# Moving small operations and sums in a fused SSM and long-convolution kernel

## The chip, the cores and the metric

The kernel runs on one NeuronCore of a Trainium2 chip. Its five engines work side by side and wait for each other through semaphores: TensorE (PE in the profile; PEld is its loading of weights), VectorE (DVE), ScalarE (ACT), GpSimd (POOL) and SyncE (SP), which only issues transfers. ACT and POOL issue transfers too. The metric is the device time of one execution in microseconds (us). Three runs of the kernel before took 380.99, 381.09 and 382.37 us, median 381.09 us.

## What is computed

The inputs are x of 2048 rows and 1024 channels, k and v of the same shape, and the parameters of two layers. Cut to what matters:

```
g = sigmoid((x * gate_w).sum(-1, keepdims=True))

# A: a diagonal complex state-space layer
Lam = Lambda_re + 1j*Lambda_im;  Lam_bar = exp(exp(log_dt) * Lam)
B_bar = ((Lam_bar - 1) / Lam)[:, None] * (B_re + 1j*B_im)
h_t = Lam_bar * h_{t-1} + B_bar x_t
a = 2 * (h C^T).real + x * Dskip

# B: a gated long convolution
k_shift[t] = sum_i k[t - i] * shift_k[:, i]      # 4 taps
kv = k_shift * v
y = irfft(rfft(pad(kv)) * rfft(pad(ssm_k)))[:2048] + kv * ssm_D
b = x * y

out = g * a + (1 - g) * b
```

Inputs and output are bf16.

## The kernel before

**The convolution (B) comes first,** in eight chunks of 128 channels. The transform is done by matmuls with cosine and sine tables (CF, SF, NCF forward, CI, SI back), and the signal is folded first: its halves are mirrored, then added and subtracted, so that the tables need half the rows. For each chunk c:

- `taps(c)`: PE makes the four-tap sums of k; ACT copies them to the tile ks (chunks from 3 on use a packed form with the small diagonals `ident2` times `pcol2`).
- `times_v(c)`: DVE multiplies ks by v; PE mirrors the first half (`mirror`); ACT copies the mirrored half to the tile lo; DVE writes ev = ks - lo; then ks + lo is made by a transfer that adds (`gather`, on POOL's queue; in chunk 1 by DVE). Each `yield` ends one step, and the caller decides what stands between two steps.
- `fold_K(c)` or `fold_columns(c)` or `mirror_K(c)`: the same folding of the filter kernel, on PE, with ACT copying the result to eok.
- `fwd_K(c)` and `fwd_V(c)`: the transforms (PE psk and psv, ACT copies to Kh and Vh; some Kh lie in the tile BT).
- `products(c)`: DVE multiplies the spectra. In the chunk loop its operations are, in order, G = Kh*Vh (128 x 4096), wkh = Kh*Vh (128 x 3072, then gathered into G), the product into BT (128 x 4096), a second wkh, and the rest with sums and differences.
- `inverse(c)`: PE psz, ACT copies to cv, which goes to a scratch in DRAM.

The loop `for c in range(NC - 1)` handles in iteration c the products of chunk c, the transforms of c + 1 and the taps and fold of c + 2. Iteration 0 is written out apart, in the branch `if c == 0`.

**The state-space layer (A) follows,** already begun in the chunk loop (`Bu`, PE both, even and odd), with scans on DVE, the matmuls with C (`Cy`, PE psy) and the sums of both layers at the end. C is turned by complex factors first: `turn_C(pi)` makes the products on ACT or DVE and sums them with DVE or, for tiles 0, 1, 4 and 5, by gathers.

**The order is written by hand.** The helper `put` ties each operation to the one before it on its engine, so the order of calls in the program is the order on PE, DVE, ACT and on the queues of SP and POOL. The set-up operations that call `nc.gpsimd` directly are not tied. Since an engine works its list in order, an operation that waits holds up all that stands behind it. PSUM is used as four rotating tiles of two banks each (`ps2`); a tile comes free when its reader, mostly ACT, is done.

**The head** is all that comes before the loop: tables, the columns of parameters (`columns`, with `pcol`, `pcol2`, `gwb` and `ident2`), chunk 0, half of chunk 1, and `state_params`, a generator of small operations on 128 x 8 tiles (th, sq, fr, invden, the sine and cosine, lam, mlam and later factors). `raise_clock` issues matmuls on zeros ahead of the first data. `lam_diag(0)` in iteration 0 uses lam and mlam on ACT.

The profile gives line 94 (in `put`) for nearly all operations, so they are told apart by the names of their tiles.

Of the kernel before, what the change touches and what calls it, by code (L numbers as in the profile page):

```python
# [9 lines left out]
ALU = mybir.AluOpType  # L10
# [10 lines left out]
def kernel(  # L21
# [26 lines left out]
    nc = tc.nc  # L48
# [34 lines left out]
    def u4(shape, dt, name):  # L83
        return s5p["wu"].tile(shape, dt, name=name, tag="u4")
# [12 lines left out]
    def mm(o, l, r, first, last):  # L97
        put("pe", nc.tensor.matmul, o, lhsT=l, rhs=r, start=first, stop=last)
# [15 lines left out]
    def copy(o, a):  # L114
        put("dve", V.tensor_copy, o, a)
# [183 lines left out]
    for k, v in enumerate((1.0, -1.0)):  # L299
        nc.gpsimd.affine_select(out=refl[:, k], in_=refl[:, k], pattern=[[1, 128]], base=-127, channel_multiplier=1,  # L300
                                compare_op=ALU.not_equal, fill=v)
    nc.gpsimd.memset(idents[:, 1:], 0.0)
    for k, v in ((1, 1.0), (2, -1.0)):
        nc.gpsimd.affine_select(out=idents[:, k], in_=idents[:, k], pattern=[[1, 128]], base=0, channel_multiplier=-1,
# [5 lines left out]
    pcol = consts.tile([128, 3 + KS, ND], F32, name="pcol")  # L310
    gwb = consts.tile([128, ND], BF16, name="gwb")
    pcol2 = consts.tile([128, 4, ND], F32, name="pcol2")
    ident2 = consts.tile([128, 64], BF16, name="ident2")
    psp = ps2([128, 2, 512], "p")
    raise_clock(3)
    for k in range(KS):
        mm(psp[:, 1, k * ND:(k + 1) * ND], skr[:, :, k], ident[32:32 + ND, 32:32 + ND], True, True)
    hf = u4([128, 2, 512], F32, "h")
    for mt in range(2):
        ts(hf[:, mt], fr_, colm[:, mt:mt + 1], None, ALU.mult)  # L320
    copy(pcol[:, 3:], psp[:, 1, 0:KS * ND].rearrange("p (i j) -> p i j", j=ND))
    dg0 = ks_pool.tile([128, KS, 128], BF16, name="dg", bufs=1)
    for k in range(KS):
        ts(dg0[:, k], ident, pcol[:, 3 + k, 0:1], None, ALU.mult)
# [2 lines left out]
    def columns():  # L327
        mm(psp[:, 0, 0:3 * ND], prow, ident[64:64 + 3 * ND, 64:64 + 3 * ND], True, True)
        copy(pcol[:, 0:3], psp[:, 0, 0:3 * ND].rearrange("p (i j) -> p i j", j=ND))
        yield  # L330
        psp2 = ps2([128, 2, 512], "p")
        mm(psp2[:, 1, KS * ND:(KS + 1) * ND], gwr, ident[32:32 + ND, 32:32 + ND], True, True)
        for q in range(4):
            for t in range(2):
                mm(psp2[t * 64:t * 64 + 64, 1, 64 + q * ND:64 + (q + 1) * ND],
                   skr[:, q // 2 * 64:q // 2 * 64 + 64, q % 2 + 2 * t], ident[32:32 + ND, 32:32 + ND], True, True)
        yield
        copy(gwb, psp2[:, 1, KS * ND:(KS + 1) * ND])
        copy(pcol2, psp2[:, 1, 64:64 + 4 * ND].rearrange("p (i j) -> p i j", j=ND))
        tt(ident2, ident[:, 0:64], ident[:, 64:128], ALU.add)  # L340

    def dgs(c, on_dve=False):
        if c >= 3:
# [66 lines left out]
    def state_params():  # L410

        dtv = small("dtv")
        act(dtv, logdt, func=ACT.Exp)
        yield
        abv = pair("abv")
        tt(abv, bc(dtv[:, None], [128, 2, NP]), pcol[:, 1:3], ALU.mult)
        yield
        act(rv, abv[:, 0], func=ACT.Exp)
        ts(thn, abv[:, 1], 1.0 / TWO_PI, None, ALU.mult)
        ts(nthn, abv[:, 1], -1.0 / TWO_PI, None, ALU.mult)  # L420
        yield
        th = pair("th")
        copy(th[:, 0], thn)
        ts(th[:, 1], thn, float(TB), None, ALU.mult)
        sq = pair("sq")
        tt(sq, pcol[:, 1:3], pcol[:, 1:3], ALU.mult)
        fr = pair("fr")
        ts(fr, th, MAGIC, -MAGIC, ALU.add, ALU.add)
        invden = small("invden")
        tt(invden, sq[:, 0], sq[:, 1], ALU.add)  # L430
        tt(fr, th, fr, ALU.subtract)
        put("dve", V.reciprocal, invden, invden)
        yield

        fa = pair("fa")
        act(fa, fr, func=ACT.Abs)
        si, co = pair("sin"), pair("cos")
        act(si, fr, func=ACT.Sin, scale=TWO_PI)
        act(co, fa, func=ACT.Sin, bias=pih, scale=-TWO_PI)
        cs["sU"], cs["cU"] = si[:, 1], co[:, 1]  # L440
        yield

        e = pair("e", 3)
        tt(lam[:, 0], rv, co[:, 0], ALU.mult)
        tt(lam[:, 1], rv, si[:, 0], ALU.mult)
        ts(mlam, lam[:, 1], -1.0, None, ALU.mult)
        yield
        tt(rv2, rv, rv, ALU.mult)
        copy(e[:, 1], lam[:, 1])
        ts(e[:, 2], lam[:, 0], -1.0, None, ALU.add)  # L450
        ts(e[:, 0], lam[:, 0], -1.0, None, ALU.add)
        p2 = pair("p2")
        tt(p2, e[:, 1:3], pcol[:, 1:3], ALU.mult)
        p1_ = th
        tt(p1_, e[:, 0:2], pcol[:, 1:3], ALU.mult)
        tt(p2[:, 0], p2[:, 0], p2[:, 1], ALU.subtract)
        tt(p1_[:, 0], p1_[:, 0], p1_[:, 1], ALU.add)
        for o, i, f in ((mc2i, p2, -2.0), (c2r, p1_, 2.0), (mc2r, p1_, -2.0)):
            put("dve", V.scalar_tensor_tensor, out=o, in0=i[:, 0], scalar=f, in1=invden, op0=ALU.mult, op1=ALU.mult)
# [220 lines left out]
    def products(c, h=0, home=u4, by_dma=True):  # L680

        if c not in GH:
            GH[c] = spectrum("G", c)
        K, Vt, G = (x[c][h].rearrange("p c b f d -> p c b (f d)") for x in (KH, VH, GH))
        w = K.shape[3]
        T2s = kv_pool.tile([128, 4096], BF16, name="t2", tag="kvh") if c == NC - 1 else BT[3].rearrange("p c d q -> p (c d q)")
        T2 = T2s[:, h * 2048:h * 2048 + 8 * w]
        W1, W2 = (WK[:, i, h * 1536:h * 1536 + 6 * w] for i in range(2))

        def mult(a, k, room, t=None):  # L690

            full = [128, 2, 4 - a, w]
            if t is None:
                t = room.rearrange("p (c b x) -> p c b x", c=2, x=w)
            tt(t, bc(K[:, k:k + 1, a:a + 1], full), Vt[:, :, 0:4 - a], ALU.mult)
            return t

        if c == 0 and h == 0:

            for f in range(2):  # L700
                k_, v_, g_ = (x[c][h][:, :, :, f] for x in (KH, VH, GH))
                tt(g_, bc(k_[:, 0:1, 0:1], [128, 2, 4, 128]), v_, ALU.mult)
        else:
            mult(0, 0, None, G)
        yield
        n1 = mult(1, 0, W1)
        if by_dma:
            gather(G[:, :, 1:], n1)
        yield
        t2 = mult(0, 1, T2)  # L710
        yield
        n2 = mult(1, 1, W2)
        if not by_dma:
            tt(G[:, :, 1:], G[:, :, 1:], n1, ALU.add)
        if c == NC - 1:
            yield
        n3 = mult(2, 1, home([128, 4 * w], BF16, "t"))
        tt(t2[:, :, 1:], t2[:, :, 1:], n2, ALU.add)
        n2 = mult(3, 1, home([128, 2 * w], BF16, "t"))
        tt(t2[:, :, 2:], t2[:, :, 2:], n3, ALU.add)  # L720
        n1 = mult(2, 0, W2[:, 0:4 * w])
        n3 = mult(3, 0, W2[:, 4 * w:])
        tt(t2[:, :, 3:], t2[:, :, 3:], n2, ALU.add)
        tt(n1[:, :, 1:], n1[:, :, 1:], n3, ALU.add)
        yield
        tt(G[:, :, 2:], G[:, :, 2:], n1, ALU.add)
        yield
        tt(t2[:, 1], G[:, 0], t2[:, 1], ALU.subtract)
        tt(t2[:, 0], G[:, 1], t2[:, 0], ALU.add)
        if c == 0 and h == 0:  # L730
            return
        lo, hi = ((t2[:, :, :, 0:256], t2[:, :, :, 256:512]) if c > 0 else
                  [T2s[:, i * 2048:(i + 1) * 2048].rearrange("p (c b x) -> p c b x", c=2, x=256) for i in range(2)])
        to = whole[c].rearrange("p (a c b x) -> p a c b x", a=2, c=2, b=4)
        tt(to[:, 0], lo, hi, ALU.subtract)
        tt(to[:, 1], lo, hi, ALU.add)
# [363 lines left out]
    step(angles)  # L1100
    step(angles)
    step(sp)
    run(first)
    dg1 = dgs(1, True)
    load("kT", 1)
# [4 lines left out]
    fwd_V(0, (0, 1))  # L1110
    step(turns)
    taps(1, dg1)
    step(columns)
    p0 = products(0, 0)
    steps(p0, 3)
    run(columns)
    step(sp)
    tv = times_v(1)
    step(tv)
    fwd_K(0, (2, 3))  # L1120
# [15 lines left out]
    for c in range(NC - 1):  # L1136
        n, nn = c + 1, c + 2
        if c == 0:
# [16 lines left out]
            fwd_K(n, (2, 3))  # L1155
            step(p1)
            step(sp)
            fwd_V(n)
            run(p1)
            run(fold_K(nn))  # L1160
            tv = times_v(nn)
            step(tv)
            load("kn", 3)
# [14 lines left out]
            step(parts)  # L1178
        step(back)
        step(tv)  # L1180
        steps(prod, 3)
        run(tv)
        step(old)
        step(tabs)
        run(back)
# [89 lines left out]
    def turn_C(pi):  # L1275
# [9 lines left out]
        for c, f in enumerate((c2r, mc2r)):  # L1285
            if by_sum:
                act(CT[pi][:, c], CT[pi][:, c], func=ACT.Identity, scale=f[:, pi:pi + 1])
            else:
                ts(CT[pi][:, c], CT[pi][:, c], f[:, pi:pi + 1], None, ALU.mult)
            if by_sum:  # L1290
                gather(CT[pi][:, c], m[c])
                yield
        if not by_sum:
            tt(CT[pi], CT[pi], whole_m, ALU.add)

    turning = [turn_C(pi) for pi in range(NP)]
# [250 lines left out]
```

## Time and profile before

| what | value |
|---|---|
| median of three runs | 381.09 us |
| the profiled execution | 381.05 us |
| its span, first to last instruction | 379.3 us |
| PE busy | 372.4 us, 2469 matmuls |
| DVE busy | 369.3 us, 595 instructions |
| ACT busy | 309.1 us, 475 instructions |
| POOL busy | 81.2 us, 111 instructions |

The span is what the profile sees; the execution is 1.75 us longer. A row of the timeline gives the start in us from the span's start, the duration, the engine, the line, the operation, the tile written, `<-`, the tiles read, shapes, and how many such instructions follow each other; in brackets stands how long the engine sat idle before, and what ended that. Consecutive operations of one engine overlap by 0.08 to 0.1 us, since a duration runs to the last write, so steps from start to start add up and durations do not. Ends of matmuls are modelled. Numbers of buffers are left out: BT stands for four tiles that are used for several things.

### The profile page before, as it was taken

Reading aid. Unit: us, or ns where it says so; the run is one execution under the profiler, and the core shown is the slowest. Engines: PE = TensorE matmul, PEld = TensorE weight load, DVE = VectorE, ACT = ScalarE, POOL = GpSimd, SP = SyncE. Lnnn points to the kernel's source line nnn. Section 1 sums busy time; section 2 is a strip of 40 time slices with the busy share of each in tenths; the row PEclk is TensorE's granted clock in tenths of the full one; section 3 lists DMA queues with packets and bytes.
Section 4 is the critical chain, followed back from the end, with each engine's and each line's share of the span. In section 5 each row is a group of like instructions: output and inputs, shape, how many; then the busy total and the mean of one; then the engine's idle time right before and its main releaser. Section 6 shows DMA issues by size and latency. Waiting matters only on the chain.

```text
span 379.3 us, 6708 instructions
## 1 busy us (share of the span) xinstructions
PE 372.4 (98%) x2469; PEld 200.1 (53%) x2469; DVE 369.3 (97%) x595; ACT 309.1 (81%) x475; POOL 81.2 (21%) x111
## 2 busy tenths in 40 slices
PE   7999999999999999999999999999999999999996
PEld 5656357575674846644454444444445444444444
DVE  8899999999999999999999999999999999999996
ACT  5879997988979999786949999996989759937611
POOL 4011030110301103031003112122414323635000
PEclk9999999999999999999999999999999999999999
DMA  7979999999999998969998999957898999899902
GB/s 168 168 115 242 234 202 193 232 209 202 194 170 213 233 207 177 174 144 152 199 200 188 200 230 257 250 111 134 155 231 174 221 251 246 145 250 164 225 2 111
DMA packets 126547, 71.78 MB, mean 189 GB/s; under 512 B 104681, under 2 KB 107633, under 8 KB 126514
## 3 DMA queue, kind: packets, MB, share of 16 engines
q1 hardware_dynamic: 112416, 45.90, 55.7%
q0 software_dynamic: 12976, 25.17, 39.2%
q10 hardware_dynamic: 1122, 0.28, 0.5%
q8 instruction: 19, 0.31, 0.3%
q14 instruction: 14, 0.11, 0.1%
HBM read 15.48 MB, written 8.39 MB: 63 GB/s over the span
## 4 chain that ended last, share of the span: by engine, by line
DVE 42%; PE 27%; DMA 14%; issue 10%; ACT 4%; POOL 2%; SPq 0%; DVEq 0%; POOLq 0%; ACTq 0%
PE both L94 16%; DVE BT L94 12%; DMA U<-Q 10%; DVE wkh L94 8%; DVE G L94 5%; DVE W L94 3%; PE psk L94 3%; PE psz L94 2%; DMA V<-Q 2%; DVE t L94 2%; DVE ks L94 2%; DVE hb L94 2%; PE psv L94 2%; PE taps L94 1%; DMA kT<-in_B_k_dram 1%
## 5 line engine op out<-in xcount | busy, mean ns | idle before, releaser
L94 PEld LDWEIGHTS <-BT 128*128 128x128 bf16 x640 | 62.1, 98 | 48.3 <-issue 0.2
L94 PE MATMUL both<-xT,BT 128*128 128x512 bf16 x384 | 83.7, 379 | 0.0
L94 POOL DMA_DIRECT2D U<-Q x26 | 26.4, 1029 | 82.3 <-ACT Q L94 40.5
L94 PEld LDWEIGHTS <-hb 128*128 128x128 bf16 x256 | 25.0, 98 | 30.2 <-issue 0.5
L94 PEld LDWEIGHTS <-U 128*128 128x128 bf16 x252 | 24.6, 98 | 27.4
L94 PE MATMUL psy<-CT,hb 128*128 128x512 bf16 x160 | 36.8, 379 | 0.0
L94 ACT ACTIVATE Vh<-psv 128x1024 bf16<-128x1024 f32 x32 | 30.7, 1032 | 5.8 <-PE psv L94 5.8
L94 PE MATMUL psy<-CT,U 128*128 128x512 bf16 (+1 forms) x160 | 35.1, 368 | 0.0
L94 ACT ACTIVATE U<-both 128x512 bf16<-128x512 f32 x44 | 24.2, 594 | 10.0 <-PE both L94 9.7
L94 DVE TENSOR_TENSOR_SCAN W<-rv,init,A 128x256 bf16<-128x256 f32 x48 | 32.1, 729 | 0.0
L94 POOL DMA_DIRECT2D G<-wkh x8 | 9.8, 1219 | 102.6 <-DVE wkh L94 102.6
L94 ACT ACTIVATE Q<-U,lam 128x512 bf16<-128x512 bf16 (+1 forms) x52 | 29.9, 612 | 0.0
L94 PE MATMUL psk<-eok,SF 128*128 128x384 bf16 (+1 forms) x120 | 28.5, 354 | 0.0
L94 PEld LDWEIGHTS <-SF 128*128 128x128 bf16 x184 | 18.0, 98 | 18.8 <-issue 0.2
L94 PE MATMUL psz<-G,CI 128*128 128x512 bf16 x64 | 24.3, 379 | 0.0
L94 PE MATMUL psz<-G,SI 128*128 128x512 bf16 x64 | 24.3, 379 | 0.0
L94 PE MATMUL psy<-CTa,hb 128*128 128x512 bf16 x96 | 22.7, 379 | 0.0
L94 PE MATMUL taps<-dg,kT 128*128 128x128 bf16 (+1 forms) x352 | 21.7, 210 | 0.7 <-DMA kT<-in_B_k_dram 0.6
L94 PEld LDWEIGHTS <-kT 128*128 128x128 bf16 x352 | 21.1, 100 | 2.3 <-DMA kT<-in_B_k_dram 1.8
L94 DVE TENSOR_TENSOR wkh<-BT,Vh 128x3072 bf16<-128x3072 bf16 (+4 forms) x20 | 21.8, 1109 | 0.0
L94 DVE TENSOR_TENSOR wkh<-Kh,Vh 128x3072 bf16<-128x3072 bf16 (+2 forms) x16 | 21.3, 1349 | 0.0
L94 PE MATMUL psy<-CTa,U 128*128 128x512 bf16 (+1 forms) x92 | 20.8, 370 | 0.0
(230 smaller groups left out, 843.5 us busy)
## 6 DMA issues: line engine op xcount, KB each, us to landing
U<-Q POOLq DMA_DIRECT2D x26, 256.0 KB, 5.1
G<-wkh POOLq DMA_DIRECT2D x6, 768.0 KB, 8.8
cv_scr<-cv SPq DMA_DIRECT2D x16, 256.0 KB, 7.7
kn<-in_B_ssm_k_dram SPq DMA_DIRECT2D x5, 512.0 KB, 4.4
v<-in_B_v_dram SPq DMA_DIRECT2D x5, 512.0 KB, 7.1
out_dram<-m SPq DMA_DIRECT2D x8, 256.0 KB, 4.2
BT<-cv_scr SPq DMA_DIRECT2D x7, 256.0 KB, 6.6
out_dram<-BT SPq DMA_DIRECT2D x7, 256.0 KB, 2.0
```

Of the source, the lines that this page charges most:

```text
L94: i = f(*a, **kw)
```

## The change

Five places are edited.

1. In the head, `ident2` is made by POOL (a memset and two affine selects) instead of a DVE sum; the eight matmuls for `pcol2` stand right behind those for `pcol`, and ACT copies the result; `gwb` is copied by ACT, and `columns` loses a step.
2. In `state_params` a new step boundary stands behind `fr`, and one more `step(sp)` follows the angles, so that th, sq and fr come before chunk 0's folding; lam is made by two operations on POOL, mlam by ACT. The first products of chunk 0 get a step boundary more, and the second wkh stands ahead of ks times v of chunk 1.
3. In iteration 0, `fold_K(2)` stands ahead of `fwd_V(1)`.
4. In iterations 1 to 6, the last step of `times_v` (ev and its gather) stands ahead of the product into BT.
5. In `turn_C`, tiles 0 and 1 are summed by one gather of 128 x 2048 each, behind both of ACT's products, instead of two of 128 x 1024.

```
+    ident2 = consts.tile([128, 64], BF16, name="ident2")
+    nc.gpsimd.memset(ident2, 0.0)
+    for k in range(2):
+        nc.gpsimd.affine_select(out=ident2, in_=ident2, pattern=[[1, 64]], base=64 * k, channel_multiplier=-1,
+                                compare_op=ALU.not_equal, fill=1.0)
...
     for k in range(KS):
         mm(psp[:, 1, k * ND:(k + 1) * ND], skr[:, :, k], ident[32:32 + ND, 32:32 + ND], True, True)
+    for q in range(4):
+        for t in range(2):
+            mm(psp[t * 64:t * 64 + 64, 1, 64 + q * ND:64 + (q + 1) * ND],
+               skr[:, q // 2 * 64:q // 2 * 64 + 64, q % 2 + 2 * t], ident[32:32 + ND, 32:32 + ND], True, True)
...
     copy(pcol[:, 3:], psp[:, 1, 0:KS * ND].rearrange("p (i j) -> p i j", j=ND))
+    act(pcol2, psp[:, 1, 64:64 + 4 * ND].rearrange("p (i j) -> p i j", j=ND), func=ACT.Copy)
...
         mm(psp2[:, 1, KS * ND:(KS + 1) * ND], gwr, ident[32:32 + ND, 32:32 + ND], True, True)
-        for q in range(4):
-            for t in range(2):
-                mm(psp2[t * 64:t * 64 + 64, 1, 64 + q * ND:64 + (q + 1) * ND],
-                   skr[:, q // 2 * 64:q // 2 * 64 + 64, q % 2 + 2 * t], ident[32:32 + ND, 32:32 + ND], True, True)
-        yield
-        copy(gwb, psp2[:, 1, KS * ND:(KS + 1) * ND])
-        copy(pcol2, psp2[:, 1, 64:64 + 4 * ND].rearrange("p (i j) -> p i j", j=ND))
-        tt(ident2, ident[:, 0:64], ident[:, 64:128], ALU.add)
+        act(gwb, psp2[:, 1, KS * ND:(KS + 1) * ND], func=ACT.Copy)
...
         ts(fr, th, MAGIC, -MAGIC, ALU.add, ALU.add)
+        yield
...
-        tt(lam[:, 0], rv, co[:, 0], ALU.mult)
-        tt(lam[:, 1], rv, si[:, 0], ALU.mult)
-        ts(mlam, lam[:, 1], -1.0, None, ALU.mult)
+        for k, o in enumerate((co, si)):
+            put("pool", nc.gpsimd.tensor_tensor, out=lam[:, k], in0=rv, in1=o[:, 0], op=ALU.mult)
+        act(mlam, lam[:, 1], func=ACT.Copy, scale=-1.0)
...
-        if c == NC - 1:
+        if c == NC - 1 or (c, h) == (0, 0):
             yield
...
     step(angles)
     step(sp)
+    step(sp)
     run(first)
...
-    step(columns)
+    run(columns)
     p0 = products(0, 0)
     steps(p0, 3)
-    run(columns)
     step(sp)
+    step(p0)
     tv = times_v(1)
...
             step(sp)
+            run(fold_K(nn))
             fwd_V(n)
             run(p1)
-            run(fold_K(nn))
...
         step(tv)
-        steps(prod, 3)
+        steps(prod, 2)
         run(tv)
+        step(prod)
         step(old)
...
-            if by_sum:
+            if pi in (4, 5):
                 gather(CT[pi][:, c], m[c])
                 yield
-        if not by_sum:
+        if pi < 2:
+            gather(CT[pi], whole_m)
+        elif not by_sum:
             tt(CT[pi], CT[pi], whole_m, ALU.add)
```

More of the change, by code (lines that the diff above doesn't have):

```diff
@@ L312 @@
     pcol2 = consts.tile([128, 4, ND], F32, name="pcol2")
-    ident2 = consts.tile([128, 64], BF16, name="ident2")
     psp = ps2([128, 2, 512], "p")
```

## The prediction

> **What bounds the kernel now.** I read the page first, for the shares of the engines.
>
> ```profile
> span 379.3 us, 6708 instructions
> ...
> PE 372.4 (98%) x2469; PEld 200.1 (53%) x2469; DVE 369.3 (97%) x595; ACT 309.1 (81%) x475; POOL 81.2 (21%) x111
> ```
>
> Two engines are full, so the waits of PE (with its weight loads, PEld) and of DVE tell which of them leads. Columns: total us, times, longest.
>
> ```profile
> PEld L94 <- DVE ks L94: 3.8, 6, 0.9
> ...
> PE mirror L94 <- DVE ks L94: 1.1, 3, 0.4
> ...
> DVE ev L94 <- PE psv L94: 0.2, 1, 0.2
> ```
>
> PE's only repeated wait is for DVE's ks (taps times v), ahead of the mirror matmuls. The timeline of PE around chunk 4's mirror shows one:
>
> ```profile
> 92.21 0.38 PE L94 MATMUL psz<-G,SI 128*128 128x512 bf16 x1
> 92.96 0.60 PE L94 MATMUL mirror<-ks,refl 128*128 128x512 bf16 x2 [0.37 <-DVE ks L94]
> ```
>
> The usual step is 0.215 us; this one is 0.75, so 0.54 is lost. The same happens at 45.96 (0.54), 138.98 (0.29) and 162.46 (0.49). From 162.46 PE runs at that step until the tail. So up to 162 DVE leads, and whatever DVE gains or loses by its ks at 161.19 arrives at the end of the kernel. DVE has no idle of 0.1 us between 28.9 and 161.
>
> Last, the timeline of DVE and then of ACT in iteration 4 of the chunk loop, where v's halves are subtracted (ev), and POOL's one small read of SBUF:
>
> ```profile
> 115.83 2.28 DVE L94 TENSOR_TENSOR G<-BT,Vh 128x4096 bf16<-128x4096 bf16 x1
> 118.03 1.75 DVE L94 TENSOR_TENSOR wkh<-BT,Vh 128x3072 bf16<-128x3072 bf16 x1
> 119.70 2.28 DVE L94 TENSOR_TENSOR BT<-BT,Vh 128x4096 bf16<-128x4096 bf16 x1
> 121.90 0.68 DVE L94 TENSOR_TENSOR ev<-ks,lo 128x1024 bf16<-128x1024 bf16 x1
> ```
>
> ```profile
> 117.06 0.90 ACT L94 ACTIVATE hr<-row,thn 128x256 f32<-128x256 f16 x2
> 117.86 0.89 ACT L94 ACTIVATE hr<-row,nthn 128x256 int32<-128x256 f16 x2
> 118.66 1.01 ACT L94 ACTIVATE cv<-psz 128x1024 bf16<-128x1024 f32 x1
> 119.56 1.02 ACT L94 ACTIVATE lo<-mirror 128x1024 bf16<-128x1024 f32 x1
> ```
>
> ```profile
> 163.55 1.10 POOL L94 COPY stamp<-xT 128x2 bf16<-128x2 bf16 x1 [12.12 <-DMA xT<-in_A_x_dram]
> ```
>
> See that ev reads lo, that lo ends at 120.58, and that the product into BT, which the change puts behind ev, begins at 119.70. That product is what now covers lo.
>
> **The change, part by part.** Times are of the profiled execution.
>
> *PE's small matmuls.* Nine p matmuls run from 20.48 to psk's start at 20.92: 0.049 each, and eight leave: 0.39 gained. They go ahead of the second clock-raising matmuls (four p took 2.71 to 2.90, so 0.38 more). The first taps move from 4.44 to about 4.56; the second half waits 0.64 for kT at 7.54 anyway. Cost 0; without that DMA, 0.12.
>
> *POOL in the head.* A memset and two affine selects more. By the rows there (memsets 0.10 to 0.60, selects 0.25 to 0.46) that is 0.6 to 1.5 ahead of the iota of row at 4.15. At 0.7, ACT's SF moves from 6.55 to about 6.6, and CF waits for DVE's h until 7.81 as before: 0. At 1.5, SF, CF, eok shift, eok's first half ends 12.45 instead of 11.65, and PE's psk moves from 12.05: 0.4 lost. I take 0, as the 128x128 selects nearest in the queue step by 0.25 and these are half as wide.
>
> *ACT's copies.* pcol2 (about 0.2) fits before row at 4.74; gwb (0.2) fits in the 1.04 idle before 22.64. Cost 0.
>
> *DVE's small operations.* gwb to fr are seven operations from 21.02 to 21.66, with 0.21 idle before and 0.08 of overlap lost: 0.93 gained. The four that stay on DVE go to 11.7, into 0.45 idle before ev at 12.26; at most 0.1 spills, and psv at 15.08 has 0.35 to spare. But DVE then meets chunk 1's ev (28.20), which already waits 0.16 for PE's psv to let go of the old ev. PE is 0.39 earlier, so DVE is too, and 0.55 is given back. The swap of ks times v with the next product keeps ks's end near 23.1; mirror needs it at 23.56. Later, lam, lam and mlam (40.02 to 40.37) leave: 0.35. DVE is 0.74 earlier at chunk 2's ks (44.69), which takes PE's mirror from 45.96 to 45.22.
>
> *lam on POOL, mlam on ACT.* lam can start when cos ends (37.36 less 0.39). Nothing like it is in the trace: 0.10 each by kT's memset, 1.10 by stamp. It must be done by 38.72, when ACT is free for mlam; behind mlam wait eok, Vh, lamd, hr, cv and lo, and behind lam on POOL kT's memset, with SP's transpose of kT at 39.26 (its reader, taps, is at 58.0). I take about 0.4 each, between these because DVE is busy, which fits by 0.9. At 1.10 each ACT slips 0.55. mlam itself is 0.11 to 0.21 (fa to sin, dtv); I take 0.12. Stamp ended at 164.65, 0.04 after DVE's two-input product did (162.32 plus 2.28, plus rounding), so it looks held rather than slow. The Trainium skill, SBUF — State Buffer, section Who interferes with whom, says that a DVE instruction with two SBUF inputs and a GpSimd instruction that reads SBUF exclude each other for a whole instruction. By that rule DVE's products of 0.4 to 1 us around 37 would each hold lam up once, which gives the same 0 as the row.
>
> *Chunk 2's fold before psv.* Same matmuls on PE. ACT is continuous from 24.15 and follows PE, 0.39 earlier. The fold starts at 37.60 and eok's second half can start 2.35 later (41.44 to 43.79 in the trace), 39.95; Vh follows psv by 1.07 (61.61 to 62.68), so 40.92, and three more at 0.905. lamd begins at 44.55, against 44.71. ACT keeps only 0.16.
>
> *ev before the BT product.* DVE now waits for lo. Let D be DVE's lateness after ev, that is lo's end plus 0.03 (a DVE start behind ACT, 18.08 to 18.11) less the old start of the BT product. Old lo end and BT start per iteration: 49.97 and 49.70; 73.58 and 73.69; 97.19 and 96.69; 120.58 and 119.70; 141.82 and 142.71; 164.13 and 166.20.
> Iteration 1: DVE comes at 48.96, lo at 49.81. D is 0.27 + 0.03 - 0.16 = +0.14: the head's 0.74 is gone. PE meets the next ks 0.14 late. Iteration 2: no wait. In iterations 3 and 4 ACT's chain to lo starts from a wait for PE (Vh at 87.87 and 113.58), so lo is as late as PE, 0.14. Iteration 3: D = 0.50 + 0.03 + 0.14 = 0.67. Iteration 4: D = 0.88 + 0.03 + 0.14 = 1.05. Iterations 5 and 6 have 0.9 and 2.1 in hand. The gather ks<-lo goes out about 2 us sooner behind G<-wkh on POOL's queue; PE shows no wait for it now (chunk 2: landed 61.28, read 62.04), so it brings nothing, and G has 2.5 us to spare (59.27, read 61.77).
>
> *C's first two tiles.* Two fewer issues of 0.9 to 1.4 us on POOL. The first landings become one, after 204.69; the second goes at about 211.6 and, with 6.6 us (CTa's transfers took 6.6 to 7.9) to 8.8 (768 KB), lands by 218.2 to 220.4; ACT wants its m again at 221.50, and psy reads the tiles at 250.1. Cost 0.
>
> **Sum.** The profiled execution took 381.05 (span 379.3 and 1.75 around it; 0.04 below the median, 381.09). PE's last mirror comes 1.05 later and all behind it: **382.1**.
>
> **Rivals.**
> 1. *The lo wait does not bite, and the head's gain arrives.* Then every ks comes 0.74 sooner: 380.3. For: three mirror waits show that DVE sets the pace. Against: ACT would have to bring lo 0.9 sooner in iteration 1 and 0.9 (plus 0.74) in iteration 4, and it has no idle to give in the chain before. It decides where lo ends before the wkh product does.
> 2. *Only chunk 1's lo is on time.* Then D enters iteration 4 at -0.74, PE and lo too, and 0.91 - 0.74 leaves +0.17: 381.2. It needs ACT 1.0 sooner at 48.97.
> 3. *lam starves on POOL.* If it gets in only in a gap of DVE, the first is near 41.1 less 0.74 (0.04 us before BT<-G,BT): two of them end near 41.0, mlam waits 2.3 and lo with it. D becomes 1.05 + 2.3: 384.4. For: stamp, 1.10 for two elements. Against: stamp got in where one product met the next, without a gap. The Trainium skill, GPSIMD Engine Reference, section Instruction dispatch, adds about 6 us for the first call of a freshly loaded kernel; no run here shows one.
>
> **How the numbers follow.** Forecast 0.58 (381.7 to 382.9: POOL's upper price gives D = 1.60, 382.65; the head's 0.4 a bit more). Rival 1 0.15, rival 2 0.13, rival 3 0.14. About 0.5% (1.9 us) is what a measurement of this kernel tells from no change: under 379.2 lies only a tail of rival 1, 0.05; over 383.0 rival 3 and a tail of the forecast, 0.17; the rest 0.78. The range, 380.0 to 383.3, leaves out rival 3 and that lower tail.
>
> **What would show it.** PE: psk at 20.5, one p before it; mirror at 45.2, then at 69.1, 93.1, 116.6, 140.0, 163.5. DVE: a wait for ACT's lo before ev of 0.9 in iteration 1, 0.5 in 3, 0.4 in 4, none in 2, 5, 6. ACT: mlam near 38.8 without a wait for POOL. I am wrong if ev shows no wait for lo in iteration 4, if mlam waits for lam, or if PE waits behind 163.5.

## The result, and the profile after

The changed kernel takes 383.37 us, median of six runs (382.95 to 384.14); the kernel before has a median of 381.85 in six (380.99 to 386.82). Some executions of every kernel here, that of before included, are disturbed and take several us longer, so the ratios given leave out the slowest runs and the experiments compare lowest times. The ratio of the two kernels is 1.0053, with a 95% interval of 1.0033 to 1.0073. A second batch gave 1.0036 (1.0001 to 1.0072). The forecast was 382.1 with a range up to 383.3, so the change costs about 1.3 us more than was forecast.

The page of the changed kernel, for the lines that were shown of the kernel before:

```profile
span 382.4 us, 6677 instructions
...
PE 372.0 (97%) x2435; PEld 200.5 (52%) x2469; DVE 369.1 (97%) x589; ACT 309.8 (81%) x478; POOL 84.5 (22%) x114
```

The work of PE and DVE is what it was; the span is 3.1 us longer than that of before. The list of waits says where it went (total us, times, longest):

```profile
PE mirror L94 <- DVE ks L94: 2.1, 6, 0.4
...
DVE ev L94 <- ACT lo L94: 1.9, 3, 1.2
...
ACT mlam L94 <- POOL lam L94: 1.1, 1, 1.1
```

The list has PE waiting for DVE's ks at six mirrors, where that of before has three. DVE waits for lo before ev in three iterations, as the prediction had it (1, 3 and 4). The third wait is the one that the prediction named as the sign that it is wrong.

PE around chunk 4's mirror, which stood at 92.96:

```profile
93.95 0.38 PE L94 MATMUL psz<-G,SI 128*128 128x512 bf16 x1
94.70 0.60 PE L94 MATMUL mirror<-ks,refl 128*128 128x512 bf16 x2 [0.37 <-DVE ks L94]
```

The stall is as long as before (0.75 for a step of 0.215), but 1.74 us later.

Iteration 4 after the change, DVE and then ACT:

```profile
118.10 2.29 DVE L94 TENSOR_TENSOR G<-BT,Vh 128x4096 bf16<-128x4096 bf16 x1
120.30 1.75 DVE L94 TENSOR_TENSOR wkh<-BT,Vh 128x3072 bf16<-128x3072 bf16 x1
122.35 0.69 DVE L94 TENSOR_TENSOR ev<-ks,lo 128x1024 bf16<-128x1024 bf16 x1 [0.30 <-ACT lo L94]
122.96 2.29 DVE L94 TENSOR_TENSOR BT<-BT,Vh 128x4096 bf16<-128x4096 bf16 x1
```

```profile
120.40 1.00 ACT L94 ACTIVATE cv<-psz 128x1024 bf16<-128x1024 f32 x1
121.30 1.01 ACT L94 ACTIVATE lo<-mirror 128x1024 bf16<-128x1024 f32 x1
```

ev starts 0.04 after lo ends (122.31), and all behind it on DVE shifts: 122.35 stands where the product into BT stood at 119.70.

Now the place where lam is made. In the kernel before it was on DVE:

```profile
39.68 0.41 DVE L94 TENSOR_TENSOR wkh<-wkh 128x512 bf16<-128x512 bf16 x1
40.02 0.16 DVE L94 TENSOR_TENSOR lam<-rv,cos 128x8 f32<-128x8 f32 x1
40.10 0.15 DVE L94 TENSOR_TENSOR lam<-rv,sin 128x8 f32<-128x8 f32 x1
40.29 0.17 DVE L94 TENSOR_SCALAR mlam<-lam 128x8 f32<-128x8 f32 x1
40.37 0.69 DVE L94 TENSOR_TENSOR G<-G,wkh 128x1024 bf16<-128x1024 bf16 x1
```

After the change, on POOL, DVE and ACT:

```profile
37.64 2.72 POOL L94 TENSOR_TENSOR lam<-rv,cos 128x8 f32<-128x8 f32 x1 [3.65 <-ACT cos L94]
40.33 0.19 POOL L94 TENSOR_TENSOR lam<-rv,sin 128x8 f32<-128x8 f32 x1
```

```profile
39.55 0.42 DVE L94 TENSOR_TENSOR BT<-BT,t 128x512 bf16<-128x512 bf16 x1
39.88 0.42 DVE L94 TENSOR_TENSOR wkh<-wkh 128x512 bf16<-128x512 bf16 x1
40.34 0.74 DVE L94 TENSOR_TENSOR G<-G,wkh 128x1024 bf16<-128x1024 bf16 x1
```

```profile
37.46 1.95 ACT L94 ACTIVATE Kh<-psk 128x1024 bf16<-128x1024 f32 x2
40.56 0.21 ACT L94 ACTIVATE mlam<-lam 128x8 f32<-128x8 f32 x1 [1.15 <-POOL lam L94]
```

Two equal products of 1024 numbers on POOL: the first takes 2.72 us, the second 0.19. DVE's products overlap their neighbours without a gap from 36 on; the first gap, 0.034 us, lies between 40.30 and 40.34, and the first lam ends at 40.36. ACT was free at 39.41 and stood idle for 1.15.

**A measure free of the head.** PE's first foldk comes anywhere between 9.00 and 10.39 us in the profiles of this study (see the last section). So marks are counted from that foldk. PE's last mirror of the chunk loop lay 152.92 us behind it before the change (162.46 - 9.54) and lies 155.06 behind it now (165.13 - 10.07): 2.14 later, where 1.05 was forecast. The profiled execution had 0.53 of later head on top, and a tail (last mirror to end) of 217.23 against 216.81, with a new wait of PE:

```profile
PE psy L94 <- ACT U L94: 0.6, 1, 0.6
```

2.14 + 0.53 + 0.42 = 3.09, the difference of the spans.

### The profile page after: what moved, and what is told of

Same layout as the page of the kernel before. It is cut to its first block, busy times and chain, and to the rows that moved or that the text cites. A ratio compares the mean times of both kernels' runs of the same rounds, so it can differ in the third digit from the quotient of the medians.

```text
span 382.4 us, 6677 instructions
## 1 busy us (share of the span) xinstructions
PE 372.0 (97%) x2435; PEld 200.5 (52%) x2469; DVE 369.1 (97%) x589; ACT 309.8 (81%) x478; POOL 84.5 (22%) x114
## 4 chain that ended last, share of the span: by engine, by line
PE 64%; DVE 21%; ACT 7%; issue 4%; DMA 1%; POOL 1%; ACTq 0%; POOLq 0%; DVEq 0%
PE psy L94 29%; PE both L94 19%; DVE BT L94 8%; DVE wkh L94 5%; PE psk L94 4%; DVE G L94 3%; PE psz L94 3%; PE taps L94 3%; PE psv L94 2%; DVE t L94 2%; PE foldk L94 2%; ACT Vh L94 1%; DVE ks L94 1%; DMA kT<-in_B_k_dram 1%; ACT m L94 1%
```

## The experiments

The table sets the lowest time of each kernel (6 to 12 runs) beside the lowest of the kernel before in the same batch (6 runs in the first, then 23 to 29), and the mark of the last mirror, counted from foldk, beside that of before. The last column is the ratio of the times to before, with its 95% interval. But for e3 (the same kernel as e7) no ratio differs from 1 by as much as 1%, so the argument rests on the marks and waits inside the profiles, and the times only agree with it.

| kernel | lowest us | against before | last mirror against before | ratio |
|---|---|---|---|---|
| changed (first batch) | 382.95 | +1.96 | +2.14 | 1.0053 (1.0033 to 1.0073) |
| e1 lam on DVE | 381.70 | +1.02 | +1.14 | 1.0010 (0.9982 to 1.0037) |
| e2 ev behind | 380.79 | +0.11 | -0.02 | 0.9966 (0.9936 to 0.9997) |
| e3 two gathers | 387.24 | +6.56 | +2.13 | 1.0195 (1.0141 to 1.0249) |
| e4 three undone | 380.53 | -0.15 | -0.32 | 0.9973 (0.9927 to 1.0019) |
| e6 ev alone | 381.76 | +1.18 | +1.25 | 1.0000 (0.9955 to 1.0045) |
| e7 two gathers again | 383.30 | +2.72 | +2.14 | 1.0065 (1.0015 to 1.0115) |
| e8 late mlam | 380.13 | -0.45 | -0.16 | 0.9954 (0.9921 to 0.9987) |
| e10 changed again | 383.01 | +2.27 | +2.12 | 1.0036 (1.0001 to 1.0072) |
| e11 lam alone | 380.97 | +0.23 | +0.33 | 0.9986 (0.9938 to 1.0034) |

**e1: lam and mlam on DVE again.** The theory is that lam's price on POOL is what the forecast missed; the rival is that its wait is covered.

```
-        for k, o in enumerate((co, si)):
-            put("pool", nc.gpsimd.tensor_tensor, out=lam[:, k], in0=rv, in1=o[:, 0], op=ALU.mult)
-        act(mlam, lam[:, 1], func=ACT.Copy, scale=-1.0)
+        tt(lam[:, 0], rv, co[:, 0], ALU.mult)
+        tt(lam[:, 1], rv, si[:, 0], ALU.mult)
+        ts(mlam, lam[:, 1], -1.0, None, ALU.mult)
```

> The changed kernel with lam and mlam on DVE again (three small products, 0.35 us of DVE), all else as changed. Theory L (POOL's lam costs 1.15 us of ACT, by the wait of mlam in the changed kernel): eok of chunk 2 follows the cosine without a wait, lo of iteration 1 ends near 50.3 instead of 51.39, ev waits 0.2 to 0.4 instead of 1.18, the last mirror of PE comes 1.0 to 1.2 sooner (165.1 to about 164.0), and the time is about 1.1 us under the changed kernel's 383.4: 382.3. Rival (lam's wait is covered, and only the place of ev costs): lo's end moves less than 0.3 and the time stays at 383.0 to 383.5.

ACT goes from Kh to eok without mlam's wait, and what is left of DVE's waits for lo is 0.46, 0.43 and 0.30:

```profile
39.52 1.02 ACT L94 ACTIVATE eok<-foldk 128x1024 bf16<-128x1024 f32 x1 [0.21 <-PE foldk L94]
40.49 2.85 ACT L94 ACTIVATE Vh<-psv 128x1024 bf16<-128x1024 f32 x3
```

```profile
DVE ev L94 <- ACT lo L94: 1.2, 3, 0.5
```

The last mirror comes at +1.14, one us sooner than in the changed kernel. The median of its twelve runs is 382.49, where 382.3 was expected. Theory L holds, with its size. e1 also is the kernel that the prediction had costed, but for DVE's three small products: forecast +1.05 to the last mirror, measured +1.14.

**e2: ev behind the product again, e6: ev ahead as the only edit.**

```
-        steps(prod, 2)
-        run(tv)
-        step(prod)
+        steps(prod, 3)
+        run(tv)
```

(e2; e6 is the reverse edit, in the kernel before.)

> The changed kernel with ev behind the product into BT again, all else as changed (lam stays on POOL). Theory L plus the cover of the product: ev waits for lo nowhere, since the product covers 2.2 us; what is left of the lateness is G's wait of 0.35 for Vh in iteration 1 and DVE's 0.03 before it, so PE's last mirror comes near 162.9 (0.4 after before's 162.46, 2.3 ahead of the changed kernel's) and the time is about 383.4 - 2.3 = 381.1. Rival (the place of ev costs nothing, the lateness comes from elsewhere): the last mirror stays near 165.1 and the time at 383.

> The kernel before with one edit: in iterations 1 to 6 ev stands ahead of the product into BT. By the sum of the prediction, without the head's gain and without lam on POOL: ev waits for lo in iterations 1, 3 and 4 and DVE's lateness after them is 0.30, 0.83 and 1.21 us; PE's last mirror comes at 163.7 instead of 162.46 and the time is 382.3 (1.2 above the kernel before). Rival (ACT is not late without the head's edits): no wait, 380.8 to 381.3.

In e2 no ev waits for lo, although lam on POOL still takes 2.72 and mlam still waits 1.15. The last mirror is where it was before the change (-0.02; the 162.9 expected, with the later head of the first profile, is -0.1 from foldk): the 0.50 that DVE gained and its wait of 0.34 for Vh, with PE's own pace, cancel. In e6 ev waits 0.22, 0.43 and 0.30, and the last mirror is 1.25 late against 1.21 expected:

```profile
DVE ev L94 <- ACT lo L94: 0.9, 3, 0.4
```

So the place of ev alone costs 1.2 us, as the prediction's arithmetic gave it.

**e11: lam on POOL as the only edit,** in the kernel before.

> The kernel before with one edit: lam on POOL, mlam on ACT. Theory H: lam takes 2.5 to 3 us there too and ends with DVE's first gap, near 41.2; mlam waits for it about 1 us and Vh and lo come later by as much; but ev stands behind the product into BT, which covers lo, so only G's wait for Vh (0.2 to 0.5) reaches DVE, against 0.18 of DVE saved: time 381.0 to 381.5, no difference that can be measured. Rival (lam on POOL is dear in itself, wherever ev stands): 382 or more.

lam takes 2.73 there, and mlam waits 1.15; the mark is +0.33 and the lowest time 0.23 above that of before. (Its profile is of an execution of 388.07 us; the mark can be used even so, since those of e3 and e7, of 387.24 and 388.40 us, put the last mirror where the changed kernel has it, within 0.01.) So lam on POOL is nearly free while ev stands behind the product into BT, which covers 2.2 us of lateness of lo, and costs 1.0 with ev ahead of it. The parts do not add: ev alone +1.25, lam alone +0.33, the head and the fold alone (e4) -0.32 make +1.26, and all together are +2.14.

**e5: why the first lam takes 2.72.** Theory F is a dear first call on POOL, theory H a hold by DVE's products. Trial products of POOL, on a tile of their own, are added to the changed kernel.

```
+    trial = consts.tile([128, 3, NP], F32, name="trial")
+    def try_pool():
+        for k in range(2):
+            put("pool", nc.gpsimd.tensor_tensor, out=trial[:, 2], in0=trial[:, k], in1=trial[:, 1], op=ALU.mult)
+    put("pool", nc.gpsimd.memset, trial, 1.0)
+    try_pool()
...
         steps(prod, 2)
+        if c in (2, 5):
+            try_pool()
         run(tv)
```

> The changed kernel with six small products added on POOL, each 128x8 f32 from and to a tile of their own that no one else uses: two in the head near 7 us, where DVE makes few two-input products, and two each behind the G<-wkh gather of iterations 2 and 5, where DVE goes from one long two-input product to the next. Theory F (POOL's first tensor product of a kernel is slow, 2.7 us, and later ones are quick): the first of the six takes about 2.7, the other five 0.2 each, and lam then takes 0.2 each, so mlam has no wait and the time falls by about 1.1 us to 382.3. Theory H (POOL's product is held while DVE's two-input products follow each other without a gap): the two in the head take 0.2 each, lam takes 2.72 again and mlam waits 1.15, and of the pairs in iterations 2 and 5 the first takes up to the rest of DVE's product, 0.5 to 4 us; the time stays at 383.2 to 383.6.

The two in the head took 0.63 and 1.18, not the 0.2 each that theory H expected: the second ran beside a two-input product of DVE and ended 0.06 behind its end, the first beside a product with a constant (see the last section). And lam, now POOL's third tensor product, took 2.72 again, so a first call is not the cause. In iteration 2 the pair took 12.2 us. POOL, then DVE in the same stretch:

```profile
76.66 12.23 POOL L94 TENSOR_TENSOR trial<-trial 128x8 f32<-128x8 f32 x2
88.84 0.89 POOL L94 DMA_DIRECT2D ks<-lo  x1
```

```profile
76.14 2.29 DVE L94 TENSOR_TENSOR BT<-BT,Vh 128x4096 bf16<-128x4096 bf16 x1
78.34 1.75 DVE L94 TENSOR_TENSOR wkh<-BT,Vh 128x3072 bf16<-128x3072 bf16 x1
...
86.28 0.69 DVE L94 TENSOR_TENSOR BT<-BT,t 128x1024 bf16<-128x1024 bf16 x1
86.89 0.69 DVE L94 TENSOR_TENSOR wkh<-wkh 128x1024 bf16<-128x1024 bf16 x1
87.61 1.22 DVE L94 TENSOR_TENSOR G<-G,wkh 128x2048 bf16<-128x2048 bf16 x1
```

The first trial of this pair runs from 76.66 to 87.64, 10.98 us, under ten products of DVE that follow each other without a gap. DVE's first gap is again 0.034 us, from 87.58 to 87.61, and the trial ends 0.06 behind the end of the product ahead of that gap. The product G<-G,wkh reads what the one before it wrote, as at 40.34 above. The products that hold a trial are not slowed: the product into BT takes 2.29 with a trial beside it and 2.29 without. What was expected of the size (0.5 to 4) was too small. The hold also shows what else it can cost: the gather ks<-lo stood behind the trials on POOL's queue, went out at 88.84, and PE stood still for it:

```profile
93.55 0.59 PE L94 MATMUL psv<-ks,SF 128*128 128x512 bf16 x2 [4.51 <-DMA ks<-lo]
```

Its runs (389.9 and more) lie 7 us above the 383 expected, and so does the last mirror: 1.15 come from the trials in the head (the iota of row, behind them on POOL, starts at 6.50 instead of 4.61), the rest with this hold. Theory H holds.

**e9: what holds POOL.** Here a, b and o are pieces of 128x1024 bf16, and `ten(f)` calls f ten times.

```
...
+    forms = [lambda: None,
+             lambda: copy(o, a),
+             lambda: ts(o, a, 2.0, None, ALU.mult),
+             lambda: put("dve", nc.vector.memset, o, 0.0),
+             lambda: tt(o, a, b, ALU.mult),
+             lambda: put("dve", V.scalar_tensor_tensor, out=o, in0=a, scalar=2.0, in1=b, op0=ALU.mult, op1=ALU.mult)]
+    for k, f in enumerate(forms):
+        ts(trial[:, k], trial[:, 6], 2.0, None, ALU.mult)
+        put("pool", nc.gpsimd.tensor_tensor, out=trial[:, 7], in0=trial[:, k], in1=trial[:, 6], op=ALU.mult)
+        ten(f)
+        ts(trial[:, 6], trial[:, 7], 0.5, None, ALU.mult)
```

> The changed kernel with a probe in the head, ahead of chunk 0's first sums: six times DVE writes 128x8 numbers, POOL multiplies them with others (128x8 f32), and DVE meanwhile goes through ten equal operations without a gap before it reads POOL's result. The ten are: none; copies 128x1024 bf16; products with a constant 128x1024 bf16; memsets; products of two tiles 128x1024 bf16; and products of two tiles with a constant (scalar_tensor_tensor). The time says nothing. If two inputs hold POOL and one does not: POOL's product takes about 0.2 in the first four and as long as the rest of DVE's row (up to ten operations, or until a boundary lets it in) in the fifth, perhaps the sixth. If every DVE operation on SBUF holds it: also in the second to fourth.

POOL's six products, in the order of the list, and the rows of DVE that go with the fifth and sixth:

```profile
9.68 0.20 POOL L94 TENSOR_TENSOR trial<-trial 128x8 f32<-128x8 f32 x1 [3.17 <-DVE trial L94]
10.44 0.24 POOL L94 TENSOR_TENSOR trial<-trial 128x8 f32<-128x8 f32 x1 [0.56 <-DVE trial L94]
15.20 0.24 POOL L94 TENSOR_TENSOR trial<-trial 128x8 f32<-128x8 f32 x1 [4.53 <-DVE trial L94]
19.97 0.20 POOL L94 TENSOR_TENSOR trial<-trial 128x8 f32<-128x8 f32 x1 [4.52 <-DVE trial L94]
26.65 0.51 POOL L94 TENSOR_TENSOR trial<-trial 128x8 f32<-128x8 f32 x1 [6.49 <-DVE trial L94]
34.07 1.04 POOL L94 TENSOR_TENSOR trial<-trial 128x8 f32<-128x8 f32 x1 [6.91 <-DVE trial L94]
```

```profile
26.42 7.22 DVE L94 TENSOR_TENSOR wkh<-wkh 128x1024 bf16<-128x1024 bf16 x10
...
33.84 2.48 DVE L94 SCALAR_TENSOR_TENSOR wkh<-wkh 128x1024 bf16<-128x1024 bf16 x2
```

Alone, and beside memsets, POOL's product takes 0.20. Beside the products of two tiles it ends 0.06 behind the end of the first of the ten, at 27.16 and 35.12. It was not held for all ten, which fits with the gaps: the ten write the same place one after the other, and a gap of 0.034 stands behind each. So this run, unlike e5, does not test a row without gaps. The memsets, too, have gaps of 0.17. Beside copies and products with a constant it took 0.24, and also ended 0.06 behind the first; these are too short (0.42) to tell a hold of 0.04 from none. The run's time, 423.8 us with the probe, says nothing more.

**e3 and e7: C's first two tiles by two transfers each.** The profile of the changed kernel showed a new stall near 253, behind the two larger transfers (they landed 9.2 and 11.2 us after issue, where the four took 7.3 to 7.9).

```
-            if pi in (4, 5):
+            if by_sum:
                 gather(CT[pi][:, c], m[c])
                 yield
-        if pi < 2:
-            gather(CT[pi], whole_m)
-        elif not by_sum:
+        if not by_sum:
```

> The changed kernel with C's tiles 0 and 1 summed by two transfers each again, all else as changed. Theory T (the larger transfer delays the loads of C's tiles 4 and 5 on SP's queue, ACT waits 0.55 at 228 and PE 0.75 at 253): the load of CT's imaginary half issues in about 2.1 us instead of 3.5, ACT has no wait for CT, PE has no stall near 253, time about 0.75 under 383.4: 382.6. Rival (the stall at 253 comes from the 2.7 us of lateness itself, since some of the transfers do not move with it): ACT's wait and PE's stall are there again, time 383.2 to 383.5.

> The same kernel as in e3_two_gathers, since that one's runs all lay at 387 us and more with a stall of PE of 3.0 us at 252, and the profiles of kernels with one transfer had 0.75, 1.03 and none there. If the stall comes by chance, with slow landings in some executions: most runs lie at 383.0 to 383.8, as those of the changed kernel, and part 5 costs nothing. If two transfers each, together with the lateness of the chunk loop, bring it regularly: all runs lie at 385 and above again.

> The changed kernel itself, beside e7_two_gathers_again. If part 5 costs nothing: most runs at 383.2 to 384.1, as those of e7, and PE's stall near 253 in this profile anything from none to 3 us, whatever the form of the sum; without it the span is 0.75 shorter than in the first profile of the changed kernel.

All runs of e3 took 387 to 391 us, and PE's wait at 252 was 2.8 us there, with the smaller transfers. In e7, the same kernel, six of twelve runs lay at 383.3 to 384.3, and in e10, the changed kernel itself beside it, eleven of twelve at 383.0 to 385.0. The profile of e10 has no such wait; that of e7, of 388.40 us, has this one:

```profile
PE psy L94 <- ACT U L94: 2.8, 1, 2.8
```

The same 2.8 stands in the profiles of e6, which has neither the larger transfers nor lam on POOL, and of e11, so part 5 is not needed for it. Theory T, as a regular cost, falls: part 5 moves the lowest time by nothing that these runs can show. One thing stays open. The stall goes with slow landings of C's first two tiles: with the larger transfers these took 6.2 to 7.8 us in e1 and e10, where PE does not wait, and 8.8 to 11.4 us in the first profile, e2, e5 and e8, where it waits 0.5 to 0.9. With two transfers each they took 6.6 to 7.9 in the kernel before and e4, without a wait, and up to 14.0 in e3, e6, e7 and e11, with the 2.8. Whether the larger transfers make slow landings more frequent is not shown.

**e4 and e8: what is left when the price is taken out.** e4 is e1, e2 and e3 in one. e8 keeps lam on POOL and puts ev back, and has mlam behind chunk 2's fold:

```
+        yield
         act(mlam, lam[:, 1], func=ACT.Copy, scale=-1.0)
...
             run(fold_K(nn))
+            step(sp)
             fwd_V(n)
...
```

> The changed kernel with lam on DVE, ev behind the product, and two transfers each, so only the head's other edits and the earlier fold are left. If the later landing of the first half of kT (5.03 instead of 4.39) was chance: DVE reaches chunk 2's ks 0.2 to 0.4 sooner than in the kernel before (44.3 to 44.5) and the time is 380.7 to 381.0. If the head's edits bring the later landing, or the later start of the taps, with them: first taps near 5.07 again, psk at 21.1, ks at 44.7 to 45.1, time 381.1 to 381.6.

> The changed kernel with ev behind the product into BT again, and mlam on ACT moved behind chunk 2's fold, so that lam on POOL has 1.9 us more before anyone waits for it. Theory L (lam on POOL costs only through mlam's wait): lam takes 2.72 as before, mlam does not wait, G of iteration 1 does not wait for Vh, PE's last mirror comes 0.4 sooner than with mlam ahead of the fold, and the time is 380.3 to 380.8, below the kernel before by 0.3 to 0.8. Rival (a POOL product under DVE's products slows DVE itself): DVE's products between 37 and 40.5 take longer than in the kernel before and the time is 381 or more.

e4 reaches chunk 2's ks 34.82 behind foldk, the kernel before 35.15: 0.33 gained by the head's edits, and the last mirror is 0.32 sooner. In e8 mlam waits for nothing, and ks of chunk 2 comes at 34.65, 0.50 sooner than before. But only 0.16 is left at the last mirror, 0.14 more than in e2 where 0.4 was expected: behind ks of chunks 4 and 5 DVE now loses 0.14 and 0.17, and PE's list has no wait for ks at a mirror between 46 and 165 (its step ahead of the last mirror is still 0.44 instead of 0.215). So with DVE half a us ahead, DVE alone no longer sets the pace. Both kernels have lower lowest times than the kernel before, by 0.15 and 0.45 us; by the marks the gain is 0.32 and 0.16 us, too little to show in the times.

## Why the prediction was wrong

Point by point, counted from foldk where marks are compared.

- *PE's small matmuls.* 0.39 forecast; psk of chunk 0's second half came 11.04 behind foldk instead of 11.38: 0.34. Right.
- *POOL in the head, ACT's copies.* Cost 0 forecast. The iota of row went from 4.15 to 4.61, less than the 0.6 to 1.5 given, but took 1.05 instead of 0.56 (see the last section), so row and SF followed later (SF at 6.76; about 6.6 was forecast). CF ran at 7.75 (7.81 before). The cost is right; the reason, the length of the new operations, was not all of it.
- *DVE's small operations.* With the p matmuls they bring ks of chunk 2 0.33 sooner (e4), against the 0.39 that the sum left of them behind chunk 1's ev. That ev waits 0.77 for psv instead of 0.16, as said. The three lam operations were put at 0.35; taking them off DVE gained 0.17 (ks of chunk 2 at 34.65 against e1's 34.82 behind foldk). The rows say why: from wkh<-wkh to G<-G,wkh there were 0.69 (39.68 to 40.37) and are 0.46 (39.88 to 40.34), since a gap comes in and the overlap is lost, and the latter product takes 0.74 instead of 0.69 with lam beside it.
- *ev before the BT product.* Waits in iterations 1, 3 and 4 and in no other, as forecast. The two later increments were forecast at 0.53 and 0.38 and came out at 0.54 and 0.39 (from ev's starts 51.42, 98.95 and 122.35 against the old 49.70, 96.69 and 119.70). Alone the edit costs 1.25 (e6; 1.21 by the same working).
- *C's first two tiles.* The four before took 7.3 to 7.9 us to land, where the prediction read 6.6 to 7.9. The two landings were later than the 8.8 us allowed (9.2 and 11.2), at 224.12 for the second, 0.04 ahead of ACT's m at 224.16. The lowest times show no cost, as forecast (383.30 in e7, 383.01 in e10); the stall of the first profile, at slow landings, was not in the forecast.
- *lam on POOL, mlam on ACT.* **This is the step that failed: the price of lam on POOL, and with it the wait of mlam, which was put at nothing.** It says: "I take about 0.4 each, between these because DVE is busy, which fits by 0.9." The first took 2.72, outside the range of 0.10 to 1.10, and mlam waited 1.15. D after iteration 1 was forecast at +0.14; it is +1.19 (41.35 behind foldk, the old product 40.16), and +0.20 in e1. The difference of 1.0 us runs through to the last mirror.

What happened is the mechanism of rival 3, which had 0.14: lam got in at DVE's first gap. The argument against it, that stamp had got in where one product met the next, took one boundary for all of them. The price of rival 3, 2.3, was too high by 1.15. It had named the gap ahead of BT<-G,BT; the gap that let lam in stands one product sooner, ahead of G<-G,wkh, where before the change lam and mlam had stood. Counted from foldk, both lam were done at 30.46 (40.53 less 10.07) and not 31.46 (41.0 less 9.54), and ACT was free 0.16 later than forecast (29.34 against 29.18). Had the sum carried the wait as measured, 1.19 for 0.14 in iteration 1, it would have been 1.05 + 1.05 = 2.1 us to the last mirror, and 383.2.

The Trainium skill, SBUF — State Buffer, section Who interferes with whom, says that whoever of DVE and GpSimd comes first has the shared access for a whole instruction. The traces agree in that a product of POOL, or the copy to stamp, ended 0.04 to 0.06 us behind the end of a DVE instruction in every case shown here in which it was held. But the prediction read this as one hold per product of 0.4 to 1 us, and there the measurement goes further: a row of products without a gap held POOL through up to ten of them. The 6 us for a first call that rival 3 named from the Trainium skill, GPSIMD Engine Reference, section Instruction dispatch, are in no run here: POOL's first tensor products took 0.63 (held, e5) and 0.20 (e9), and neither stood behind a pause: the first started as POOL's operation before it ended, the second 0.08 behind the DVE operation that it waited for.

## What to carry to other kernels

A small operation moved to POOL can be held for as long as DVE goes from one two-input product to the next: look for DVE's first real gap behind the operation's inputs, and reckon with that as its end, whatever its size. It may get in sooner (the last section has cases), but a plan should not rest on that. Ask next who waits for it and who is queued behind it on POOL, transfers above all. And two edits that each use up the same cover must be costed together: here the lateness of lo was free until ev was moved out from behind the product that hid it.

## What the runs showed of the hardware that was not expected

- POOL's product of 128x8 took 0.19 to 0.20 us when free and 10.98 when held by ten products of DVE in a row; a gap of 0.034 us lets it in. In iteration 5 of e5, trials also got in where one product overlapped the next by 0.08 (they took 1.83 and 1.60), and the copy to stamp (1.10 before, 2.08 after) did so too. Which boundaries without a gap do this stays open.
- A product with a constant, one input of 128x1024 f32 (rq), seems to hold POOL as well: the first trial of e5 took 0.63 beside it and ended 0.06 behind its end. The iota of row, which reads no tile, fits: in every profile with the new head but e5 it started behind rq's start and took 1.05. With the old head (before, e6, e11) it started first, and rq took 1.10 instead of 0.82, so there DVE was the slower one. Rows of the kernel before, then of the changed one:

```profile
4.15 0.56 POOL L261 IOTA row_i<- 128x512 int32 x1
4.16 1.10 DVE L94 TENSOR_SCALAR rq<-h 128x1024 f32<-128x1024 f32 x1
```

```profile
4.61 1.05 POOL L261 IOTA row_i<- 128x512 int32 x1
4.38 0.82 DVE L94 TENSOR_SCALAR rq<-h 128x1024 f32<-128x1024 f32 x1
```

- The head varies: with the same operations in it, the changed head had its first foldk at 9.06 to 10.39, that of before at 9.00 to 9.54. kT's first half landed between 3.96 and 5.19 us, and PE's step from tap to tap fell from 0.106 to some 0.056 us as early as 4.8 and as late as 8.1. The 0.53 of later head in the profile of the changed kernel is within this spread. Whether it is chance is not fully settled: the two kernels that were profiled twice came out at 10.07 and 10.39, and at 9.11 and 9.10. But the fastest run of the changed kernel, 382.95, leaves at most about 9.3 for its foldk if the rest took no less than in the profiles (an estimate: 382.95 less 1.78 around the span, 155.05 to the last mirror and 216.81 behind it).
